# Weights of a fused attention and gated-unit kernel: float32 loads on SyncE's queue with casts on GpSimd in place of casting transfers, under another written order

## The chip, the cores and the metric

The kernel runs on one core of a Trainium2 chip. The metric is the device time of the program in microseconds (us): before the change 173.61, the median of three runs (173.09 to 173.88). Lower is better.

## The reference

Two stages follow each other. The first is causal attention for 4 batches, 8 heads, 768 positions and head size 64. Keys are grouped in chunks of 32, and each query keeps only the six chunks with the highest upper bound of its score:

```
ub = sum(max(q*k_min, q*k_max), axis=-1)       # for every query and chunk
top_chunks = argsort(ub)[..., -6:]             # causal chunks only
scores = where(chunk in top_chunks and causal, q@k.T / 8, -1e9)
attn = softmax(scores) @ v
```

The second stage takes the attention output, joined over the heads to x of [4, 768, 512], through a causal convolution of five taps per channel, which gives a gate, and through two 512 by 512 weights:

```
gate = sigmoid(sum(conv_w[k] * shifted(x, k) for k in range(5)))
out = (gate * (x @ w_val)) @ w_out
```

All inputs and the output are float32.

## The kernel before

**Tiles and stages.** Two heads are one pair, so there are 16 pairs p, and four pairs make a batch b. For each pair, K and Q are loaded (`Lk`, `Lq`, two transfers each) and transposed on TensorE (`KT`, `QT`); ScalarE copies them out of PSUM as float16 (`KE` L661, `QH` L701); VectorE reduces the chunk bounds (`KX` L672), and GpSimd prepares them (`KB`, `KS`, L680 to L697). TensorE multiplies the bounds (`CF`, `BD` L776), VectorE finds the sixth largest (`T8` L784, `CM` L791), and the mask reaches the score layout through a transposing DMA on SyncE's queue (`MD` L807) or, for the first pairs, through TensorE (`MT`). The scores of a pair are six blocks (`S` L819 to L824), each with two exponentials on ScalarE (`E` L828, 192 in all); GpSimd cuts the causal triangles (`A` L839) and casts V to float16 (`VC` L760); TensorE multiplies with V (`AV` L848), and VectorE normalises (`RC` L854, `NR` L864 or L870).

**The second stage.** The normalised rows are transposed for the second stage by a DMA on SyncE's queue (`XT` L890; pairs 0, 1 and 15 through TensorE). For the first two pairs of a batch the convolution is done on TensorE (`CV` L942), for the other two by five taps per pair (`TP`: the first on ScalarE, L925, four on VectorE, L928). `TH` (L932, L947) is the gate's tanh on ScalarE. `VL` is x @ w_val on TensorE, in a first half from the weights `wv` (L963) and a second, `z`, from `wvn` (L956). `GV` (L968) multiplies gate and value on VectorE, `OU` (L976) multiplies with the weights `wo`, `OE` (L984 on ScalarE, L986 on VectorE) copies the result into one of eight buffers `OSB` of 128 by 512 float32, and `ST` (L989) stores it.

**The weights.** They lie in SBUF as float16 and are loaded once, by twelve transfers from GpSimd's queue that cast while they move: `wval` (four, L1072) fills the lower 64 partitions of `wv`, `wvn` (four, L1066), and `wout` (four, L1081 and L1084). Two more transfers on SyncE's queue, `wvd0` and `wvd1` (L1075), copy the lower half of `wv` to the upper 64 partitions:

```
g.op("SP", 430, 430, f"wvd{j}", lambda js=js: nc.sync.dma_start(
    out=wval_sb[HP[1], js, 0:DM], in_=wval_sb[HP[0], js, 0:DM]),
     [("wv", 0, j, 0), ("wv", 0, j, 1)], [("wv", 1, j)], (), dma=700.0)
```

**What sets the order.** Nothing is scheduled when the program is built: each operation has a name, and `ORDER` (L110), a list of 1507 names written out in the file, is the order in which they are emitted. Every engine, and every engine's DMA queue, works through its share of that list strictly in turn and waits at the first operation whose inputs are not there. The transfers of SyncE's queue use eight semaphores in rotation, so each also waits until the eighth transfer before it has landed. The names `F` and `G` with a number are filler products on TensorE, without use for the result, that run while the first loads are on their way.

Of the kernel before, what the change touches and what calls it, by code (L numbers as in the profile page):

```python
# [110 lines left out]
Lk0.1 mfz F5 F14 F11 G6 mKB0 F13 cwl G11 G7 F7 F8 Lk0.0 F9 F6 ident identh G19 G2 G12 G15 KT0.1  # L111
KX0.10 KT0.0 KX0.00 G18 F0 mNS1 KX0.01 KX0.11 Lq0.1 QT0.1 QF0.1 mKF0 KF0.10 KF0.11 cwn0 F15 KF0.01
RF0.1 Lk2.0 cwn1 G14 cwt F4 em0 Lq0.0 cws F10 F12 Lk1.0 KF0.00 G16 G8 cfill ident2 QH0.1 KT2
KX2.11 identb CF0 BF0.3 T80.3 KE2.0 QT0.0 QF0.0 KX2.10 mNS0 KE2.1 G17 em1 G13 KX2.01 BF0.4 KX2.00
Lq2.0 BF0.5 T80.5 G5 T80.4 Lq1.0 G9 KE0.1 CM0.4 CM0.3 F2 QH0.0 KB2.0 KS2 KB2.1 KB2.2 CM0.5 dg01
KT1 KX1.00 RF0.0 BF0.2 em2 BF0.1 KX1.10 KX1.11 T80.2 mVA0 KE0.0 G3 G4 QT2 KE1.0 G0 T80.1 CM0.1 F3
KE1.1 CM0.2 Lk3.0 KX1.01 KB1.0 KS1 KB1.1 G10 F1 G1 QH2.1 QL2.1 MT0 ME0 QH2.0 QL2.0 dg03 RH2 QT1
QH1.0 mKB1 KB2.3 QL1.0 QH1.1 S0.5 E0.05 E0.15 S0.4 E0.14 KB1.2 KB1.3 E0.04 QL1.1 RH1 Lq3.0 S0.2
E0.12 S0.3 E0.13 Lk4.0 A0.4 Lv0 KT3 KB1.4 E0.02 S0.0 E0.10 CF1 BD1.5 BD1.4 BD1.2 KX3.10 BD1.3
E0.03 KX3.00 BD1.1 dg02 S0.1 CF2 KX3.11 KB2.4 BD2.2 BD2.1 T81.1 BD2.5 BD2.4 T81.3 E0.00 QT3 E0.01  # L120
E0.11 T81.5 A0.1 T81.4 KE3.1 T81.2 CM1 T82.4 QH3.0 KX3.01 KB3.0 KB3.1 MT1 ME1 QH3.1 Lq4.0 T82.5
KE3.0 S1.5 S1.4 A0.5 Lv1 E1.15 A0.3 KS3 KB3.2 KB3.4 QL3.0 E1.05 E1.04 Lv2 BD2.3 S1.1 QL3.1 RH3
E1.14 mVA1 KB3.3 E1.11 T82.3 Lk5.0 S1.3 E1.03 VC0 T82.2 T82.1 CM2 KT4 KX4.10 KX4.00 E1.13 S1.2
E1.12 A1.3 E1.01 KX4.01 KX4.11 S1.0 KB4.0 CF3 BD3.5 E1.10 VC1 BD3.2 Lq5.0 BD3.3 KE4.0 BD3.4 BD3.1
T83.1 A1.1 AV0.00 AV0.04 AV0.03 Lv3 T83.5 MT2 ME2 A1.4 KE4.1 KS4 mxT T83.4 AV0.12 T83.2 AV0.15
T83.3 AV0.10 AV0.11 AV0.05 AV0.13 AV0.14 RC0.1 AV0.02 AV0.01 RC0.0 E1.00 E1.02 A1.5 mVA2 CM3 S2.5
E2.15 E2.05 NR0.0 NR0.1 QT4 QH4.0 QL4.0 QH4.1 S2.1 Lk6.0 QL4.1 E2.11 E2.01 RH4 KB4.1 S2.3 E2.03
AV1.10 AV1.02 AV1.11 AV1.13 AV1.14 AV1.01 AV1.12 VC2 AV1.00 AV1.04 AV1.15 RC1.1 E2.13 AV1.03 S2.0
Lv4 NR1.1 KT5 E2.10 KX5.00 KX5.10 Lq6.0 A2.1 E2.00 KX5.11 S2.4 E2.04 E2.14 S2.2 KB4.2 E2.02 AV1.05
MT3 KB4.4 RC1.0 ME3 NR1.0 KE5.1 E2.12 KB4.3 CF4 BD4.1 BD4.2 BD4.3 XT0 XTE0 dg00 BD4.4 BD4.5 T84.5  # L130
S3.5 E3.15 E3.05 T84.3 Lk7.0 S3.1 E3.11 QT5 QH5.0 S3.2 A2.5 A2.3 A2.4 T84.4 AV2.05 AV2.02 T84.1
T84.2 KX5.01 CM4 KB5.0 KS5 AV2.01 AV2.04 E3.12 E3.02 QL5.0 AV2.03 AV2.00 RC2.0 KE5.0 E3.01 AV2.13
AV2.12 NR2.0 AV2.10 AV2.11 AV2.14 AV2.15 RC2.1 XT1 XTE1 S3.4 QH5.1 S3.3 NR2.1 E3.04 E3.03 XT2
# [6 lines left out]
AV3.05 E4.10 AV3.02 KX7.00 KX7.10 KB7.0 T86.5 KS7 T86.1 AV3.03 T86.2 QT7 RC3.0 T86.3 KB7.1 wvd0  # L140
T86.4 AV3.12 E4.13 QH7.1 A4.4 NR3.0 KB7.2 AV3.15 A4.5 AV3.11 AV3.10 AV3.14 QH7.0 KB7.4 CM6 KE7.1
KB7.3 QL7.1 AV3.13 RC3.1 QL7.0 KE7.0 NR3.1 S5.0 E5.00 wout0 S5.3 E5.13 XT3 RH7 E5.10 VC4 S5.1
E5.11 wvn3 TP2.4 KT8 S5.5 E5.05 E5.15 CF7 BD7.1 BD7.4 BD7.3 E5.01 T87.1 T87.4 E5.03 S5.4 E5.04
KX8.00 E5.14 S5.2 E5.02 E5.12 A4.3 AV4.15 KX8.11 KX8.10 MD6 AV4.14 BD7.5 BD7.2 AV4.10 AV4.13
AV4.12 KE8.1 KX8.01 Lk9.0 AV4.11 A5.5 T87.5 AV4.05 AV4.04 AV4.03 Lk10.0 RC4.1 T87.3 T87.2 AV4.01
AV4.02 KB8.0 KS8 TP3.0 KE8.0 AV4.00 NR4.1 RC4.0 VL0.1 A5.3 CM7 MD7 NR4.0 A5.4 TP3.1 QT8 QH8.0
QH8.1 VL0.1z GV0.11 GV0.10 TH2 S6.1 E6.01 QL8.1 QL8.0 S6.4 E6.04 VC5 A5.1 AV5.14 AV5.10 E6.14
AV5.15 AV5.03 AV5.11 AV5.01 AV5.02 AV5.13 AV5.04 Lq9.0 AV5.00 AV5.05 RC5.0 RH8 wout2 S6.5 E6.05
KB8.1 KB8.2 KB8.4 E6.15 A6.5 E6.11 wout3 Lq10.0 AV5.12 RC5.1 S6.3 E6.13 NR5.0 S6.0 E6.03 S6.2
E6.02 E6.12 TP3.2 NR5.1 TP3.3 VL0.2 VL0.2z GV0.20 E6.00 TP3.4 S7.3 E6.10 E7.13 A6.3 KT9 KX9.10  # L150
VL0.3 KX9.11 E7.03 GV0.21 TH3 S7.0 E7.00 wout1 VL0.3z CF8 KE9.1 KB8.3 BD8.2 BD8.4 BD8.1 GV0.30
# [998 lines left out]
```

## Time and profile before

| | us |
|---|---|
| median of three runs (lowest, highest) | 173.61 (173.09, 173.88) |
| the profiled execution, its own time | 173.19 |
| span of its trace, first to last instruction | 171.5 |
| busy: TensorE, VectorE, ScalarE, GpSimd | 159.6, 145.7, 145.3, 99.2 |
| granted TensorE clock | 0.999 of full speed |
| SyncE's queue: share of 16 DMA engines, MB | 79.7%, 29.96 |
| GpSimd's queue: share of 16 DMA engines, MB | 4.4%, 1.06 |

All times come from one profiled execution and count from the span's start. A row of the timeline gives start, duration, engine, source line, what is written from what, the number of instructions in the row, and, in brackets, how long the engine stood idle before it and what ended that. PE is TensorE, ACT ScalarE, DVE VectorE, POOL GpSimd, SP SyncE; SPq and POOLq are the instruction queues that issue transfers. The chain of waits follows the work that ended last back through whatever released each step; it is inferred from semaphore events. A busy TensorE is not a TensorE at its peak, since its products are pipelined.

### The profile page before, as it was taken

How to read it: one execution, taken by the hardware profiler on the slowest of the kernel's cores; microseconds unless marked ns; L12 is line 12 of the kernel's file. 1: busy time of each engine (PE TensorE's matmuls, PEld its weight loads, DVE VectorE, ACT ScalarE, POOL GpSimd, SP SyncE). 2: the span in 40 equal slices, each digit the busy share in tenths (PEclk: the TensorE clock that was granted, in tenths of full speed). 3: DMA queues.
4: the chain of work that ended last, by engine and by line, in shares of the span. 5: the costliest groups of instructions: out<-in, count | busy, mean ns of one | idle time of the engine just before them, and what ended most of it. 6: DMA issues, size and time to landing. Idle time of an engine off the chain costs nothing.

```text
span 171.5 us, 7644 instructions
## 1 busy us (share of the span) xinstructions
PE 159.6 (93%) x3118; PEld 106.7 (62%) x3118; DVE 145.7 (85%) x434; ACT 145.3 (85%) x320; POOL 99.2 (58%) x218
## 2 busy tenths in 40 slices
...
GB/s 98 222 271 190 268 252 268 230 64 99 216 143 194 177 196 209 257 134 201 165 202 150 214 254 204 185 129 184 202 113 237 272 185 2 74 85 207 166 191 237
DMA packets 98578, 31.50 MB, mean 184 GB/s; under 512 B 94187, under 2 KB 95467, under 8 KB 98544
## 3 DMA queue, kind: packets, MB, share of 16 engines
q1 hardware_dynamic: 97424, 29.96, 79.7%
q0 software_dynamic: 1120, 1.06, 4.4%
...
q14 instruction: 10, 0.08, 0.2%
...
## 4 chain that ended last, share of the span: by engine, by line
PE 40%; ACT 21%; DVE 16%; POOL 8%; DMA 7%; issue 3%; SPq 2%; POOLq 0%; ACTq 0%
ACT P L828 14%; PE ps L976 10%; DVE G L928 7%; PE ps L848 6%; PE ps L821 4%; PE ps L963 4%; PE ps L956 4%; PE ps L824 4%; PE ps L647 3%; DMA xT<-ON 3%; DVE GV L968 3%; ACT KE L661 3%; DMA QM<-NS 2%; POOL P L839 2%; DVE KK L672 2%
## 5 line engine op out<-in xcount | busy, mean ns | idle before, releaser
L828 ACT ACTIVATE P<-ps 128x512 f16<-128x512 f32 (+1 forms) x192 | 89.7, 582 | 5.0 <-PE ps L824 3.1
L839 POOL TENSOR_SCALAR_AFFINE_SELECT P<-P 128x256 f16<-128x256 f16 (+1 forms) x64 | 37.0, 591 | 21.5 <-ACT P L828 19.9
L824 PE MATMUL ps<-QM,EM 64*128 64x512 f16 (+4 forms) x256 | 36.6, 290 | 1.0 <-DMA QM<-NS 0.7
L672 DVE TENSOR_REDUCE KK<-ps 128x12 f32<-128x384 f32 x64 | 31.9, 547 | 4.8 <-PE ps L639 3.8
L821 PE MATMUL ps<-QHL,KE 64*128 64x512 f16 (+4 forms) x256 | 35.0, 292 | 0.2
L928 DVE SCALAR_TENSOR_TENSOR G<-xT,cwT,G 128x768 f32<-128x768 f16 x32 | 34.0, 1081 | 1.3 <-ACT G L925 1.2
L848 PEld LDWEIGHTS <-P 128*128 128x128 f16 x672 | 24.3, 98 | 8.7 <-issue 5.0
L848 PE MATMUL ps<-VA,P 128*128 128x65 f16 x672 | 27.8, 194 | 0.8 <-DVE GV L968 0.4
L976 PE MATMUL ps<-wo,GV 128*128 128x512 f16 (+1 forms) x100 | 23.1, 371 | 0.0
L821 PEld LDWEIGHTS <-KE 64*128 64x128 f16 x256 | 13.2, 94 | 7.9 <-issue 3.7
L661 ACT ACTIVATE KE<-ps 128x384 f16<-128x384 f32 x32 | 16.3, 550 | 0.9 <-DVE KK L672 0.9
L784 DVE MAX8 TOP<-ps 128x8 f32<-128x20 f32 (+4 forms) x160 | 15.6, 164 | 1.4 <-PE ps L776 1.4
L984 ACT ACTIVATE OSB<-ps 128x512 f32<-128x512 f32 (+1 forms) x22 | 13.0, 615 | 4.2 <-PE ps L976 4.2
L968 DVE SCALAR_TENSOR_TENSOR GV<-G,ps 128x384 f16<-128x384 f32 x32 | 16.2, 544 | 0.2
L760 POOL CAST VA<-vn 128x768 f16<-128x768 f32 x16 | 14.7, 916 | 3.0 <-DMA vn<-in_v_dram 2.9
L701 ACT ACTIVATE QHL<-ps 128x384 f16<-128x384 f32 x32 | 15.3, 537 | 0.8 <-PE ps L821 0.6
L824 PEld LDWEIGHTS <-EM 64*128 64x128 f16 x256 | 12.3, 94 | 4.3 <-issue 2.9
L741 DVE SCALAR_TENSOR_TENSOR QHL<-ps,QHL 128x320 f16<-128x320 f32 x30 | 13.6, 478 | 1.4 <-ACT QHL L701 1.4
L976 PEld LDWEIGHTS <-GV 128*128 128x128 f16 x100 | 8.7, 97 | 9.7 <-DVE GV L968 1.0
L776 PE MATMUL ps<-KB,RHL 128*128 128x48 f16 x225 | 13.2, 183 | 1.0 <-DVE RHL L748 0.5
L776 PE MATMUL ps<-KB,QHL 128*128 128x48 f16 x225 | 13.2, 183 | 0.0
L963 PE MATMUL ps<-xT,wv 64*128 64x384 f16 x128 | 13.1, 323 | 0.1
...
## 6 DMA issues: line engine op xcount, KB each, us to landing
...
```

Of the source, the lines that this page charges most:

```text
L661: nc.scalar.activation(out=spread(KE[p % 3], p, w), in_=bank(gr, None), func=AF.Copy)
L672: nc.vector.tensor_reduce(out=o, in_=i, axis=AX.X, op=ALU.min if mx else ALU.max)
L776: nc.tensor.matmul(out=o, lhsT=lt, rhs=kb[:, j, :], start=False, stop=(n == 5), skip_group_check=True)
L821: nc.tensor.matmul(out=pq[hh][:, col + a:col + n], lhsT=KE[p % 3][HP[hh], ks], rhs=QH[p % 3][HP[hh], q0 + a:q0 + n], start=True, stop=False)
L824: nc.tensor.matmul(out=pq[hh][:, col + a:col + n], lhsT=EM[HP[hh], ks], rhs=qm[HP[hh], q0 + a - 128:q0 + n - 128], start=False, stop=True)
L828: e.EX = lambda p, hh, bi, tot, gr: nc.scalar.activation(out=PT[hh, bi, p % 2][:, 0:tot], in_=bank(gr, None)[:, 0:tot], func=AF.Exp, scale ...
L839: nc.gpsimd.affine_select(out=ap, in_=ap, pattern=[[0, 2], [0, n], [1, 128]], compare_op=ALU.is_ge, fill=0.0, base=0, channel_multiplier=-1)
L848: nc.tensor.matmul(out=pav[:, qt, :], lhsT=PT[a, bi, p % 2][:, col:col + 128], rhs=VA[p % 3][:, hh, jt, :], start=(jt == 0), stop=(jt == qt))
L928: en.scalar_tensor_tensor(out=GT[sl], in0=x, scalar=w, in1=GT[sl], op0=ALU.mult, op1=ALU.add)
L963: nc.tensor.matmul(out=pv[h], lhsT=wval_sb[HP[h], gi, ws], rhs=xT[HP[h], (b % 2) * 2, gi, :, LD:LD + 128], start=(gi == 0), stop=False)
L968: e.GV = lambda b, et, w, gr: nc.vector.scalar_tensor_tensor(out=GVT[(b % 2) * NCT + et][:, w * HB:(w + 1) * HB], in0=GT[(b % 2) * NCT + e ...
L976: nc.tensor.matmul(out=po[:, 0:z - a], lhsT=GVT[(b % 2) * NCT + et][:, s * 128:(s + 1) * 128], rhs=wout_sb[:, et, a:z], start=(et == 0), s ...
```

## The change

The casting transfers and the two copies are gone. Ten loads on SyncE's queue bring the weights as float32, 256 KB each, into the buffers `OSB`, which hold nothing until the first output rows are ready, and ten casts on GpSimd write the float16 tiles. `WLa` (four loads) bring the part of w_val for `wv` twice, into the lower and the upper 64 partitions, and `CWa0` to `CWa3` cast it; `WLn` and `CWn` (two each) do `wvn`; `WLo` and `CWo` (four each) do `wo`, the last two of them in buffers that `CWa0` and `CWa1` have emptied. The first half of `VL` now waits for all four `CWa`, every `OU` for all four `CWo`. `wv` loses 32 unused columns, the eight `OSB` become one tile with eight parts, and `XT` and `XTE` must now follow `mxT`, which clears four columns ahead of each row.

```
-            g.op("SP", 430, 430, f"wvd{j}", lambda js=js: nc.sync.dma_start(
-                out=wval_sb[HP[1], js, 0:DM], in_=wval_sb[HP[0], js, 0:DM]),
...
+        def stage(name, out, in_, slots):
+            g.op("SP", 430, 430, name, lambda: nc.sync.dma_start(out=out, in_=in_), (),
+                 [("osb", i, a) for i in slots for a in (0, 256)], (), dma=700.0)
+
+        def cast(name, out, slot, key):
+            g.op("POOL", 600, 650, name, lambda: nc.gpsimd.tensor_copy(out=out, in_=OSB[slot]),
+                 [("osb", slot, 0), ("osb", slot, 256)], [key], ())
...
+        for x in range(2):
             for r in range(2):
+                rows = slice(64 * x + 32 * r, 64 * x + 32 * r + 32)
+                g.op("SP", 430, 430, f"WLa{x}{r}", lambda rows=rows, r=r: nc.sync.dma_start(
+                    out=OSBT[rows, 0:NG], in_=wsrc[r][:, 0:NG]), (), [("wst", x, r)], (), dma=700.0)
+        for n in range(NG):
+            g.op("POOL", 600, 650, f"CWa{n}", lambda n=n: nc.gpsimd.tensor_copy(
+                out=wval_sb[:, n], in_=OSB[n]), [("wst", x, r) for x in range(2) for r in range(2)],
+                 [("wv", n), ("osb", n, 0), ("osb", n, 256)], ())
+        for r in range(2):
+            stage(f"WLn{r}", OSB[NG + r], moe_w_val[256 + 128 * r:][0:128], [NG + r])
+            cast(f"CWn{r}", wval_nat[:, r], NG + r, ("wvn", r))
+        for j in range(NCT):
...
+            slot = (6, 7, 0, 1)[j]
+            stage(f"WLo{j}", OSB[slot], rows, [slot])
+            cast(f"CWo{j}", wout_sb[:, j], slot, ("wo", j))
```

The list `ORDER` is another one throughout, with 1513 names. Two of its new lines:

```
+BF0.2 KX1.00 KE2.0 QH0.0 F7 KE1.1 WLn1 KS2 KE1.0 QT2 KB2.2 KB2.3 T80.2 T80.1 CM0.2 F11 QH2.0 CM0.1
+MT0 QT1 QH2.1 KX1.10 ME0 G6 S0.2 QH1.1 Lv0 QH1.0 KX1.01 KB1.0 KB1.1 QL2.0 Lq3.0 E0.02 QL1.1 QL2.1
```

Three places of it follow, engine by engine as the built programs have them. The changed file's lines stand one lower than the old ones from L630 to L1056 (the transposes are L806 and L889 there); L1064 is `stage`, L1068 `cast`, L1078 `CWa`.

SyncE's queue around the transpose of pair 3, `XT3`, written from ON_133 to xT, with the mask transpose of pair 6 (QM_90) behind it. Names in brackets are the semaphores that a transfer waits for: DMAHW the eighth transfer before it, DMASW GpSimd's transfers, PE, DVE and Pool the engines. Before:

```order
L1075 DMA wv_66<-wv_66 64x2x512 [waits DMAHW1_49,DMASW2_49,DMASW1_49]
L1075 DMA wv_66<-wv_66 64x2x512 [waits DMAHW2_49,DMASW5_49,DMASW3_49]
L890 DMA_TRANSPOSE xT<-ON_133 128x6x128 [waits DMAHW3_49,DVE_49]
L807 DMA_TRANSPOSE QM_90<-NS_114 128x5x128 [waits DMAHW4_49,PE_49]
L630 DMA kn_76<-in_k_dram 128x6x64 [waits DMAHW5_49]
```

Now:

```order
L1064 DMA OSB<-in_moe_w_out_dram 128x512 [waits DMAHW6_49]
L629 DMA kn_77<-in_k_dram 128x6x64 [waits DMAHW7_49,PE_49]
L629 DMA kn_77<-in_k_dram 128x6x64 [waits DMAHW0_49]
L625 DMA vn_85<-in_v_dram 128x12x64 [waits DMAHW1_49,Pool_49]
L625 DMA vn_84<-in_v_dram 128x12x64 [waits DMAHW2_49]
L889 DMA_TRANSPOSE xT<-ON_133 128x6x128 [waits DMAHW3_49,DVE_49]
L1064 DMA OSB<-in_moe_w_out_dram 128x512 [waits DMAHW4_49,Pool_49]
L806 DMA_TRANSPOSE QM_90<-NS_114 128x5x128 [waits DMAHW5_49,PE_49]
```

The two copies that waited for GpSimd's transfers ahead of `XT3` are replaced by loads; behind `XT3` stands a load, `WLo3`, that waits for GpSimd (for the cast `CWa1`), and the mask of pair 6 stands behind that.

GpSimd from the bounds of pair 7 (KK_105) to the last triangle of pair 4 (the P_0 tiles). Before, with the last of the `wvn` transfers and the first `wout`:

```order
L680 TENSOR_TENSOR KK_105<-KK_105 128x24
L695 TENSOR_SCALAR KQ_107<-KK_105 128x48
L684 TENSOR_SCALAR KC_109<-KK_105 128x48
L839 AFFINE_SELECT P_0_120<-P_0_120 128x2x128
L697 TENSOR_TENSOR KC_109<-KQ_107,KC_109 128x48
L839 AFFINE_SELECT P_0_121<-P_0_121 128x256
L692 COPY KB_111<-KC_109 64x4x24 x2
L1084 DMA wo_68<-in_moe_w_out_dram 64x1024
L760 CAST VA_95<-vn_83 128x12x64
L1066 DMA wvn<-in_moe_w_val_dram 64x512
L839 AFFINE_SELECT P_0_119<-P_0_119 128x2x256
```

Now:

```order
L679 TENSOR_TENSOR KK_105<-KK_105 128x24
L694 TENSOR_SCALAR KQ_107<-KK_105 128x48
L683 TENSOR_SCALAR KC_109<-KK_105 128x48
L696 TENSOR_TENSOR KC_109<-KQ_107,KC_109 128x48
L691 COPY KB_111<-KC_109 64x4x24
L838 AFFINE_SELECT P_0_119<-P_0_119 128x2x256
L838 AFFINE_SELECT P_0_121<-P_0_121 128x256
L1078 CAST wv_66<-OSB 128x512 x2
L691 COPY KB_111<-KC_109 64x4x24
L838 AFFINE_SELECT P_0_117<-P_0_117 128x4x128
L1078 CAST wv_66<-OSB 128x512 x2
```

The four `CWa` casts stand between the parts of pair 7's bounds and the triangles of pair 4, where transfers were issued before.

ScalarE around the first tap of pair 3 (`TP3.0`, which reads what `XT3` wrote). Before, behind the last exponential of pair 5:

```order
L828 ACTIVATE P_1_124<-ps_1760 128x512
L661 ACTIVATE KE_89<-ps_1703 128x6x64
L925 ACTIVATE G_137<-xT,cwT 128x768
L661 ACTIVATE KE_89<-ps_1702 128x6x64
L701 ACTIVATE QHL_99<-ps_1863 128x6x64
L701 ACTIVATE QHL_99<-ps_1864 128x6x64
L932 ACTIVATE G_136<-G_136 128x768
```

Now:

```order
L827 ACTIVATE P_1_126<-ps_1714 128x512
L660 ACTIVATE KE_89<-ps_1687 128x6x64
L827 ACTIVATE P_1_125<-ps_1722 128x512
L700 ACTIVATE QHL_99<-ps_1843 128x6x64
L700 ACTIVATE QHL_99<-ps_1842 128x6x64
L924 ACTIVATE G_137<-xT,cwT 128x768
L931 ACTIVATE G_136<-G_136 128x768
```

The tap moved behind one more copy of K and both copies of Q.

More of the change, by code (lines that the diff above doesn't have):

```diff
@@ L110 @@
 ORDER = """
[L111 to L133, printed above, removed]
@@ L140 @@
[L140 to L151, printed above, removed]
@@ L206 @@
-ST3.0 OU3.2 OE3.2 ST3.2 OU3.3 OE3.3 ST3.3 OU3.4 OE3.4 ST3.4 OU3.5z OE3.5z ST3.5z OU3.5 OE3.5 ST3.5
+cwl Lk0.1 mKB1 Lk0.0 mfz mxT F12 G11 F13 F10 G5 G14 F4 G9 F9 ident identh F3 G17 F5 cfill Lq0.1
+F15 G16 KT0.1 KT0.0 KX0.11 ident2 mNS0 G12 Lk2.0 KE0.1 cwn0 QT0.1 QF0.1 RF0.1 G7 F8 Lq0.0 QH0.1
+KX0.10 cwn1 KX0.01 cwt F6 mKF0 KX0.00 KF0.10 Lk1.0 cws mKB0 KF0.00 F1 KT2 F14 KF0.01 KF0.11 KX2.10
+KX2.11 Lq2.0 KX2.00 Lq1.0 KE0.0 identb CF0 BF0.3 BF0.5 BF0.4 mVA0 KE2.1 T80.5 T80.3 T80.4 QT0.0
+QF0.0 CM0.3 em0 em1 CM0.5 F2 CM0.4 dg00 em2 G3 KX2.01 KB2.0 F0 KB2.1 KT1 RF0.0 BF0.1 Lk3.0 KX1.11
```

185 lines of the change are left out of this document (98 added, 87 removed).

## The prediction, made before the change had run

> **What bounds the kernel now.** I read the page first, then the list of waits, the chain, and the timelines of single engines where the chain leaves TensorE and ScalarE.
>
> ```profile
> span 171.5 us, 7644 instructions
> PE 159.6 (93%) x3118; PEld 106.7 (62%) x3118; DVE 145.7 (85%) x434; ACT 145.3 (85%) x320; POOL 99.2 (58%) x218
> 40.00:50.00 10.00, 8.57 (x295) 6.27 (x295) 9.41 (x26) 9.68 (x24) 8.54 (x19) 1.00 1.01 183
> 50.00:60.00 10.00, 9.07 (x191) 6.80 (x188) 8.87 (x39) 8.83 (x21) 9.33 (x21) 1.00 0.91 166
> ```
>
> No engine is the bound by itself: three are filled to 85% or more, so a bubble that they share is the thing to look for. The two rows by stage (us, then busy PE, PEld, DVE, ACT, POOL, the clock, DMA) show one: between 40 and 60 us GpSimd, elsewhere at 58%, is busy 8.54 and 9.33 of 10, and the others have holes. Here is the chain of waits (start, length, what) in that stretch, cut:
>
> ```profile
> 44.50 0.58 POOL wv L1072
> 47.57 0.51 POOL wv L1072
> 48.50 0.49 POOL wvn L1066
> 48.99 0.55 POOL wv L1072
> ...
> 54.88 4.74 DMA xT<-ON
> 59.64 0.94 ACT G L925
> ```
>
> It runs through the very transfers that the change removes, to XT3, and from there to the tap TP3.0 on ScalarE. Why XT3 starts at 54.88 is in SyncE's queue, in its waits, and in the row of VectorE that completes XT3's input:
>
> ```profile
> 50.78 4.00 SPq L1075 DMA_DIRECT2D wv<-wv  x2
> 54.88 1.78 SPq L890 DMA_TRANSPOSE xT<-ON  x1
> 56.75 1.23 SPq L807 DMA_TRANSPOSE QM<-NS  x1
> SPq L1075 <- DMA wv<-in_moe_w_val_dram: 2.6, 1, 2.6
> 52.69 0.54 DVE L864 TENSOR_TENSOR ON<-ps,RCP 128x384 f16<-128x384 f32 x1
> ```
>
> The rows of pair 3 are ready at 52.69 + 0.54 = 53.23, but the queue is held by the second weight copy, which waits 2.6 us for a casting transfer from GpSimd and is issued only by 54.78. XT3 starts 54.88 - 53.23 = 1.65 us late, and its transfer lands at 59.62. Who pays:
>
> ```profile
> 59.64 0.94 ACT L925 ACTIVATE G<-xT,cwT 128x768 f32<-128x768 f16 x1 [1.06 <-DMA xT<-ON]
> 60.61 1.28 DVE L928 SCALAR_TENSOR_TENSOR G<-xT,cwT,G 128x768 f32<-128x768 f16 x1 [0.92 <-ACT G L925]
> 61.01 0.26 PE L819 MATMUL ps<-QHL,KE 64*128 64x192 f16 x2 [0.61 <-ACT KE L661]
> ```
>
> ScalarE idles 1.06 us, VectorE 0.92 us behind it, TensorE 0.61 us: one bubble on all three, and it hangs on the two copies.
>
> **The change part by part.** *The copies go.* With no wait for GpSimd in SyncE's queue, XT3 can be issued when its rows are ready, 1.65 us earlier, more than the 1.06 us that ScalarE waits; in the new order TP3.0 also stands behind three further copies on ScalarE. So the bubble closes: -1.06 us. Next late there is XT3's own length: 53.23 + 4.74 = 57.97, against a ScalarE that reaches the tap at 59.64 - 1.06 = 58.58.
>
> *GpSimd.* Transfers out, casts in:
>
> ```profile
> L760 POOL CAST VA<-vn 128x768 f16<-128x768 f32 x16 | 14.7, 916 | 3.0 <-DMA vn<-in_v_dram 2.9
> L1072 POOL DMA_DIRECT2D wv<-in_moe_w_val_dram x4 | 2.4, 600 | 0.0
> L1066 POOL DMA_DIRECT2D wvn<-in_moe_w_val_dram x4 | 2.1, 537 | 0.0
> L1081 POOL DMA_DIRECT2D wo<-in_moe_w_out_dram x2 | 1.3, 626 | 0.0
> L1084 POOL DMA_DIRECT2D wo<-in_moe_w_out_dram x2 | 1.1, 574 | 0.0
> ```
>
> Removed: 2.4 + 2.1 + 1.3 + 1.1 = 6.9 us. No cast of 128x512 is in the trace; the nearest row is the cast of V, 916 ns for 768 columns, so 0.61 us by columns (0.54 us if it is no cheaper than an issued transfer, 0.92 us if width does not matter). Ten are 6.1 us (5.4 to 9.2). GpSimd's sum is thus almost unchanged; what changes is that nobody on SyncE waits for it, and that the casts are spread from pair 1 to pair 7. I take 0, from -0.5 to +1.0 us.
>
> *SyncE's queue and the DMA engines.* Two copies less, ten loads more. By shape a load is 256 KB, 2.5 MB in all, for 1.06 MB of casting transfers and 0.25 MB of copies before, over 31.5 MB. Where a load stands ahead of work with spare time it costs nothing. The place with least spare is the start, where WLn1 and Lv0 now stand ahead of Lq3, the Q of pair 3:
>
> ```profile
> 12.06 1.30 SPq L630 DMA_DIRECT2D qn<-in_q_dram  x2
> 16.27 0.59 SPq L626 DMA_DIRECT2D vn<-in_v_dram  x1
> DMA to landing us min/median/max: 2.3/3.5/6.3
> 20.50 0.58 PE L647 MATMUL ps<-ident,qn 64*128 64x64 f32 x12
> ```
>
> Lq3 (12.06) and the next load up to Lv0 (16.27) are four issues in 4.21 us, 1.05 each. Two more ahead make Lq3 2.1 us later: issued by 12.06 + 1.30 + 2.1 = 15.46, landed 3.5 to 6.3 later, 18.96 to 21.76 (median and maximum of the Q loads). Its transposes began at 20.50, so the cost is 0 by the median, +1.3 us at worst. I take 0.
>
> *The new wait.* The first half of VL needs all four CWa, and the scores of pair 6 stand behind VL on TensorE, their exponentials behind those. From the new order, after VectorE has the bounds of pair 7:
>
> ```profile
> 48.30 1.94 DVE L672 TENSOR_REDUCE KK<-ps 128x12 f32<-128x384 f32 x4
> L680 POOL TENSOR_TENSOR KK<-KK 128x24 f32<-128x24 f32 x15 | 3.8, 251 | 14.4 <-DVE KK L672 14.1
> L692 POOL COPY KB<-KC 64x96 f16<-64x96 f16 x30 | 10.9, 365 | 1.4
> L839 POOL TENSOR_SCALAR_AFFINE_SELECT P<-P 128x512 f16<-128x512 f16 x32 | 23.0, 724 | 7.5 <-ACT P L828 6.5 <-POOL P L839 0.6
> L839 POOL TENSOR_SCALAR_AFFINE_SELECT P<-P 128x256 f16<-128x256 f16 x32 | 14.6, 458 | 14.0 <-ACT P L828 13.5
> 58.45 0.82 PE L963 MATMUL ps<-xT,wv 64*128 64x384 f16 x8
> ```
>
> The bounds end at 50.24. Then come six small operations (0.25 to 0.37, say 2.0 in all), two wide triangles (1.45), a narrow one (0.46) and four casts (2.44): 50.24 + 6.35 = 56.6. VL began at 58.45, so 1.8 us are left: cost 0 as long as the casts are not held up.
>
> *The written order* moves everything else too. Up to about 45 us ScalarE is full and its queue keeps the same content, so I expect nothing there. Behind 60 us the trace bounds what other waits can give or take:
>
> ```profile
> ACT P L828 <- PE ps L824: 3.1, 5, 1.1
> ACT P L828 <- POOL KB L692: 1.3, 1, 1.3
> ```
>
> That is 4.4 us of waits of the exponentials. An order can remove a part or add as much; I take 0, with 1.0 us either way. `XT` behind `mxT`, the dropped columns and the joined OSB are free: nothing in the new order waits more for them, since mxT now stands at the start.
>
> *Sum*, on the profiled execution, 1.69 us of whose 173.19 lie around the span: 173.19 - 1.06 = 172.13. That execution is 0.42 under the median of the three runs; from the median the sum is 172.55. I put 172.4 between them.
>
> **The rivals.** *The copies were not all that held it (about the same).* For: TensorE waited only 0.61 us, and behind 62 us the chain is mostly products. If TensorE's bubble is what counts, 173.19 - 0.61 = 172.58, with the same allowance of 0.27 for the median 172.85. Against: VectorE waited 0.92 us for the same cause and is as full as ScalarE.
>
> *The casts are held up (slower).* Small copies on GpSimd take long beside a tap on VectorE, while an issued transfer did not:
>
> ```profile
> 42.28 0.26 POOL L692 COPY KB<-KC 64x96 f16<-64x96 f16 x1
> 46.08 1.00 DVE L928 SCALAR_TENSOR_TENSOR G<-xT,cwT,G 128x768 f32<-128x768 f16 x1
> 46.18 1.02 POOL L692 COPY KB<-KC 64x96 f16<-64x96 f16 x1
> 47.31 1.07 DVE L928 SCALAR_TENSOR_TENSOR G<-xT,cwT,G 128x768 f32<-128x768 f16 x1
> 47.51 0.56 POOL L1072 DMA_DIRECT2D wv<-in_moe_w_val_dram  x1
> ```
>
> The copy of 0.26 us takes 1.02, until just past the tap's end at 47.08; the transfer inside the next tap takes 0.56, about its mean. So the change swaps work that is not held for work that may be. If each CWa loses up to a tap, 1.0 us, the last ends at 56.6 + 4.0 = 60.6, VL starts 2.2 us late, and TensorE and ScalarE with it: 173.19 - 1.06 + 2.2 = 174.3, with the allowance 174.6. It decides from 58.4 on. Against: three of the four taps of pair 2 stand ahead of the bounds of pair 7 in the new order, so the casts meet one tap, or two. [...]
>
> *More goes (faster).* If the new order also saves a quarter of the 4.4 us, 1.1 us, it is 172.4 - 1.1 = 171.3.
>
> **How the numbers follow.** A measurement of this kernel tells about 0.5% from no change, 0.87 us, so "faster" is under 172.74 and "slower" over 174.48. The forecast, the bubble closed and little else, has 0.44: 0.36 of it faster, 0.08 the same, since its edge of a few tenths reaches 172.74. TensorE's bubble alone has 0.20, the same. More gain has 0.11, faster. The held casts, with the late Lq3 as a smaller case of its kind, have 0.25: 0.22 slower, 0.03 the same. Faster 0.47, same 0.31, slower 0.22. The range takes in the two outer rivals, 171.3 and 174.6, and leaves what lies beyond them, about two in ten: 171.2 to 174.6. The likeliest case alone spans 171.9 to 172.9.
>
> **What would show it.** Right: no wait of SyncE's queue for GpSimd's transfers, XT3 issued within 0.3 us of its rows, no wait of TP3.0 over 0.3 us, casts of 0.55 to 0.70 us, VL not waiting for a cast. Wrong: VL or OU waiting for GpSimd; the transposes of pair 3's Q waiting for their load; casts of 1 us and more; or TP3.0 on time and the waits of ScalarE and TensorE behind 60 us grown by the same microsecond.

## The result and the profile after

The change made the kernel slower. Before: median 173.19 us (172.68 to 175.51, 20 runs). After: median 176.82 us (173.33 to 181.91, 20 runs). The ratio is 1.0113, with a 95% interval of 1.0076 to 1.015. After's runs lie 5% apart and before's 1.6%, and the ratio leaves out every run more than 1.5% above its kernel's fastest (it keeps five of after's twenty), so the medians of all runs stand beside it here and below.

The profiled execution of after is its fastest, 173.33 us, hardly over the 173.19 us of before's. It shows where after stops, not all that its usual runs lose; two of those follow under after_again_1 and after_again_2. The page, with DMA queues as packets, MB and share of 16 engines:

```profile
span 171.6 us, 7644 instructions
PE 160.9 (94%) x3118; PEld 108.6 (63%) x3118; DVE 145.7 (85%) x434; ACT 145.3 (85%) x320; POOL 99.6 (58%) x216
...
q1 hardware_dynamic: 98576, 32.32, 88.4%
```

The engines have as much work as before (TensorE 1.3 us more, at a clock of 0.987). What has grown is SyncE's DMA queue: 88.4%, where both data queues together had 84.1% (79.7 and 4.4). The stages, in the columns of the prediction:

```profile
40.00:50.00 10.00, 8.04 (x257) 5.25 (x252) 8.60 (x24) 8.91 (x22) 6.96 (x13) 0.89 1.01 217
50.00:60.00 10.00, 9.88 (x223) 7.49 (x219) 8.91 (x40) 9.26 (x23) 5.76 (x13) 0.94 1.12 228
```

The hole has moved forward: 40 to 50 us now holds 257 products where 295 stood, at a clock of 0.89. The place that the prediction looked at is mended, here in the timeline (VectorE's normalising row, `XT3`, the last casts `CWa2` and `CWa3`, the next `MD`, the first half of `VL`, `TP3.0`, then TensorE and ScalarE behind it):

```profile
54.95 0.55 DVE L863 TENSOR_TENSOR ON<-ps,RCP 128x384 f16<-128x384 f32 x1
55.53 1.54 SPq L889 DMA_TRANSPOSE xT<-ON  x1
55.70 1.16 POOL L1078 CAST wv<-OSB 128x512 f16<-128x512 f32 x2
57.82 1.20 SPq L806 DMA_TRANSPOSE QM<-NS  x1
59.41 0.89 PE L962 MATMUL ps<-xT,wv 64*128 64x384 f16 x8
60.38 1.12 ACT L924 ACTIVATE G<-xT,cwT 128x768 f32<-128x768 f16 x1
62.53 0.39 PE L823 MATMUL ps<-QM,EM 64*128 64x512 f16 x2 [1.15 <-DMA QM<-NS]
63.00 1.09 ACT L827 ACTIVATE P<-ps 128x512 f16<-128x512 f32 x2 [0.78 <-PE ps L823]
```

The rows are ready at 55.50 and `XT3` is issued at 55.53; the tap has no bracket, so ScalarE did not wait for it. But the rows themselves come 2.3 us later than before, and behind the tap there is a new wait of TensorE, 1.15 us for a mask (`MD6`), with one of 0.78 us on ScalarE behind it. The larger stop lies earlier, where SyncE's queue carries three of the four `WLa` (the first went out at 32.67), V of pair 4, K of pair 8 and Q of pair 7:

```profile
40.16 1.05 SPq L1075 DMA_DIRECT2D OSB<-in_moe_w_val_dram  x2
41.31 0.39 SPq L625 DMA_DIRECT2D vn<-in_v_dram  x1
41.73 1.58 SPq L1075 DMA_DIRECT2D OSB<-in_moe_w_val_dram  x1
43.36 1.75 SPq L629 DMA_DIRECT2D kn<-in_k_dram  x2
45.16 3.44 SPq L629 DMA_DIRECT2D qn<-in_q_dram  x2
47.70 0.88 PE L646 MATMUL ps<-ident,kn 64*128 64x64 f32 x12 [1.39 <-ACT P L827]
47.81 0.90 POOL L759 CAST VA<-vn 128x768 f16<-128x768 f32 x1 [1.19 <-DMA vn<-in_v_dram]
```

TensorE stands for 1.39 us ahead of K's transposes of pair 7, GpSimd 1.19 us for V, and issuing the two loads of `Lq7` takes 3.44 us. Some transfers land later: the medians from issue to landing are 5.4 us for V, 3.5 for `XT` and 4.1 for `MD`, where the same view of before has 4.8, 2.8 and 3.4. Only V's goes with the loads. old_path_new_order below, which has the new order without them, reads 4.8, 3.5 and 4.3, and the loads of K and Q of 192 KB land no later than before (3.7 and 3.9 us against 3.9 and 4.2).

### The profile page after: what moved, and what is told of

It reads as the page before. It is cut to its first block, busy times and chain, and to the rows that moved or that the text cites. A ratio compares the mean times of both kernels' runs of the same rounds, so it can differ in the third digit from the quotient of the medians.

```text
span 171.6 us, 7644 instructions
## 1 busy us (share of the span) xinstructions
PE 160.9 (94%) x3118; PEld 108.6 (63%) x3118; DVE 145.7 (85%) x434; ACT 145.3 (85%) x320; POOL 99.6 (58%) x216
## 3 DMA queue, kind: packets, MB, share of 16 engines
q1 hardware_dynamic: 98576, 32.32, 88.4%
## 4 chain that ended last, share of the span: by engine, by line
PE 50%; DVE 19%; ACT 15%; DMA 9%; issue 3%; SPq 1%; DVEq 0%
ACT P L827 10%; PE ps L975 8%; DVE G L927 6%; PE ps L820 6%; PE ps L847 6%; DMA QM<-NS 5%; PE ps L823 5%; PE ps L955 5%; PE ps L962 4%; PE ps L646 4%; PE ps L775 3%; DVE KK L671 3%; DMA xT<-ON 3%; PE ps L941 2%; DVE TOP L783 2%
## 5 line engine op out<-in xcount | busy, mean ns | idle before, releaser
L827 ACT ACTIVATE P<-ps 128x512 f16<-128x512 f32 (+1 forms) x192 | 91.1, 577 | 6.8 <-PE ps L823 6.7
L838 POOL TENSOR_SCALAR_AFFINE_SELECT P<-P 128x512 f16<-128x512 f16 (+1 forms) x64 | 37.5, 599 | 27.2 <-ACT P L827 26.2
L823 PE MATMUL ps<-QM,EM 64*128 64x512 f16 (+4 forms) x256 | 38.1, 293 | 1.9 <-DMA QM<-NS 1.9
L820 PE MATMUL ps<-QHL,KE 64*128 64x512 f16 (+4 forms) x256 | 35.9, 295 | 0.9 <-DVE QHL L740 0.9
L927 DVE SCALAR_TENSOR_TENSOR G<-xT,cwT,G 128x768 f32<-128x768 f16 x32 | 34.7, 1104 | 0.3
L820 PEld LDWEIGHTS <-KE 64*128 64x128 f16 x256 | 13.8, 96 | 7.0 <-issue 2.9
L783 DVE MAX8 TOP<-ps 128x8 f32<-128x12 f32 (+4 forms) x160 | 15.3, 162 | 1.4 <-PE ps L775 1.0
L775 PE MATMUL ps<-KB,RHL 128*128 128x48 f16 x225 | 13.9, 184 | 0.4 <-DVE TOP L783 0.4
L775 PE MATMUL ps<-KB,QHL 128*128 128x48 f16 x225 | 13.8, 184 | 0.0
L775 PEld LDWEIGHTS <-RHL 128*128 128x128 f16 x225 | 11.5, 97 | 3.0 <-issue 2.3
```

What stands on the lines that cost most here:

```text
L775: nc.tensor.matmul(out=o, lhsT=lt, rhs=kb[:, j, :], start=False, stop=(n == 5), skip_group_check=True)
L783: nc.vector.max(out=TOP[p % 2][:, it - 1, s, :], in_=bank(gr, None)[:, it - 1, s * NCH:s * NCH + n])
L820: nc.tensor.matmul(out=pq[hh][:, col + a:col + n], lhsT=KE[p % 3][HP[hh], ks], rhs=QH[p % 3][HP[hh], q0 + a:q0 + n], start=True, stop=False)
L823: nc.tensor.matmul(out=pq[hh][:, col + a:col + n], lhsT=EM[HP[hh], ks], rhs=qm[HP[hh], q0 + a - 128:q0 + n - 128], start=False, stop=True)
L827: e.EX = lambda p, hh, bi, tot, gr: nc.scalar.activation(out=PT[hh, bi, p % 2][:, 0:tot], in_=bank(gr, None)[:, 0:tot], func=AF.Exp, scale ...
L838: nc.gpsimd.affine_select(out=ap, in_=ap, pattern=[[0, 2], [0, n], [1, 128]], compare_op=ALU.is_ge, fill=0.0, base=0, channel_multiplier=-1)
```

## The experiments

Where an edit only moves names in `ORDER`, the diff shows the names around the place. Each ratio is against before, run beside it on the same chip. Where medians of two jobs are compared, before's own median differs between them, from 172.82 to 173.42 us.

### Which part: bubble, order or weight path

**old_path_copies_later.** Before, with the two copies behind `XT3`.

```
-AV3.00 wvd1 AV3.05 ... KB7.1 wvd0 T86.4 ... XT3 RH7
+AV3.00 AV3.05 ... KB7.1 T86.4 ... XT3 wvd1 wvd0 RH7
```

> The kernel before, with only its two copies wvd1 and wvd0 moved on SyncE's queue to just behind XT3, so that XT3 no longer waits behind a copy that waits for GpSimd's casting transfers; nothing else is changed. Theory of the prediction (the shared bubble at 58.6 to 61 us is on every engine's path): XT3 is issued 1.6 us earlier, the tap TP3.0 waits no more, and the time falls by 0.9 to 1.2 us, to 172.0 to 172.3 beside 173.2. Rival (only TensorE's 0.6 us was on the path, or the gain is given back at the next transfer): 172.6 to 173.2.

Median 173.94 us, ratio 1.0062 (1.0038 to 1.0086). Its timeline at `XT3`, `TP3.0` and `VL`:

```profile
53.40 2.11 SPq L888 DMA_TRANSPOSE xT<-ON  x1
58.56 0.96 ACT L923 ACTIVATE G<-xT,cwT 128x768 f32<-128x768 f16 x1
60.22 0.82 PE L961 MATMUL ps<-xT,wv 64*128 64x384 f16 x7 [1.30 <-DMA wv<-wv]
```

The bubble closes as the prediction worked out (`XT3` 1.5 us earlier, the tap at 58.56 without a wait), and the gain is given back at once: `VL` waits 1.30 us for the copy that now comes last. The time even rises, from 172.99 to 173.94, so no price of the bubble can be read from this run.

**new_path_old_order.** After's loads and casts put into before's order, each near the transfer that it replaces.

```
-S3.1 ... wval10 ... wval11 ... wval01 ... wval00 wvn2
+WLa11 S3.1 ... WLa01 ... WLa00 ... WLa10 ... CWa0 ... CWa1 ... CWa2 CWa3
```

> The kernel after with the written order of the kernel before: the ten float32 loads stand in SyncE's queue and the ten casts on GpSimd, but every other instruction stands where it stood before. Theory O (the new written order costs the time): 171.9 to 172.9, as the prediction had it for the weight path alone, with runs within 1% of each other and a granted clock of 0.99 or more. Theory Q (ten more loads in SyncE's queue hold up its other transfers, by more or less from run to run): 175 to 178, with runs that differ by 2% or more, as the kernel after.

Median 180.5 us, ratio 1.0449 (1.0425 to 1.0473). GpSimd's timeline shows why it says nothing about the order:

```profile
50.86 0.61 POOL L1076 CAST wv<-OSB 128x512 f16<-128x512 f32 x1 [5.97 <-DMA OSB<-in_moe_w_val_dram]
```

The casts stood too early, and GpSimd, with the bounds of the next pairs behind it, waited 5.97 us for a load. It does show what a cast costs that waits on GpSimd.

**old_path_new_order.** After's order with before's transfers and copies.

```
-XTE1 A3.4 ... CM5 E4.00 ... S4.3 CF6 ... Lv5 AV3.14
+XTE1 wval10 A3.4 ... CM5 wval11 E4.00 ... S4.3 wval00 wvn2 CF6 ... Lv5 wvd1 wvd0 AV3.14
```

> The kernel before (casting transfers on GpSimd, two copies on SyncE) with the written order of the kernel after; the transfers stand between the instructions beside which they stood before, the two copies ahead of XT3. Theory O: 175 to 178 with runs that differ by 2% or more, as the kernel after, and KT7 waits on TensorE at 47 us. Theory Q: 172 to 174 with runs within 1%.

Median 173.04 us (171.25 to 174.26), ratio 0.9979 (0.9948 to 1.001). So the order alone costs nothing, and what after loses comes with the weight path. Its stages read

```profile
40.00:50.00 10.00, 8.51 (x286) 5.85 (x284) 8.66 (x27) 9.56 (x23) 9.25 (x19) 1.00 1.13 184
50.00:60.00 10.00, 9.04 (x187) 6.33 (x184) 9.35 (x39) 8.89 (x22) 6.63 (x15) 1.00 1.18 229
```

with DMA shares (1.13 and 1.18) above those of after (1.01 and 1.12): a full share by itself did not make this kernel slow. Its queue at the place of the stop, for comparison (Lk8, then Lq7):

```profile
40.43 1.78 SPq L628 DMA_DIRECT2D kn<-in_k_dram  x2
42.26 1.28 SPq L628 DMA_DIRECT2D qn<-in_q_dram  x2
```

**kt7_behind_s43.** After, with K's transposes of pair 7 behind the next scores, since these had their inputs.

```
-S4.4 KT7 KX7.10 WLo0 S4.3 CF6
+S4.4 WLo0 S4.3 KT7 KX7.10 CF6
```

> The kernel after with pair 7's key transposes (KT7) and the reduction KX7.10 put behind pair 4's score products S4.3 instead of ahead of them. Theory O in its narrow form (TensorE's wait of 1.39 us for a PSUM bank at KT7, with S4.3 behind it, and the stretch of lower granted clock that follows): 1.0 to 2.5 us less than the kernel after, 174 to 176 in the median, and the granted clock stays at 1.00 from 40 to 60 us. Rivals (the wait moves to the next bank, or the spread comes from the loads in SyncE's queue): within 0.5 us of the kernel after, runs still 2% and more apart.

Median 176.3 us, ratio 1.0157 (1.0112 to 1.0202). The list of waits of TensorE:

```profile
PE ps L817 <- ACT P L826: 1.7, 1, 1.7
```

The stop did not go with the transposes. It stayed at the same place in TensorE's stream, now ahead of `S4.3`, 1.72 us long. So neither K nor Q of pair 7 was what TensorE stood for there (the last section comes back to it).

### Where the four WLa stand

**wla_early.** All four at the first one's place; `Lq8` later, to make room.

```
-RC1.0 WLa11 NR1.0 Lq8.0 S3.1 ... MD5 E4.10
+RC1.0 WLa11 WLa01 WLa00 WLa10 NR1.0 S3.1 ... MD5 Lq8.0 E4.10
```

> The kernel after, with the four loads WLa taken out of the stretch from 40 to 46 us: three of them follow the first in SyncE's queue, at 33 to 36 us, where Lq8 stood, and Lq8 goes behind MD5, to 49 us. What the runs so far show: with the old weight path the new order takes 173.0 us and TensorE's clock stays at 1.00; in the kernel after, and in the one with KT7 behind S4.3, TensorE stops at the same place of its stream of instructions (its 1729th record of the trace, whichever instruction stands there) with its semaphores long reached, starts again 1.2 to 1.4 us after a 16 KB transfer of the instruction queue has landed, and the granted clock is 0.5 for the next 3.4 us. Theory I (the WLa loads hold up the transfer that brings TensorE's instructions, while 160 short products of the convolution use up the instructions at hand; the stop costs 1.3 us and the halved clock some 1.7 us): the instruction transfer that starts at 45.5 us after starts by 44 us, no stop of over 0.5 us at 46 us, clock 1.00, median 172.5 to 174.0 and runs within 1.5%. Rival Q (it is the count and the bytes of the loads, wherever they stand, that delay the mask and row transfers): 175.5 to 177.5 with runs 2% and more apart.

**wla_late.** Three of them behind `MD5`.

```
-E3.14 WLa01 ... E3.03 WLa00 ... KB6.0 WLa10 ... MD5 E4.10
+E3.14 ... E3.03 ... KB6.0 ... MD5 WLa01 WLa00 WLa10 E4.10
```

> The kernel after, with three of the four loads WLa (01, 00, 10) put behind MD5 in SyncE's queue, at 49 to 52 us; their casts stay at 53.5 us and later. Theory I: the instruction transfer starts by 44 us, no stop of TensorE at 46 us, clock 1.00, Lv4 lands earlier and VC4 doesn't wait, median 172.5 to 174.0 and runs within 1.5%, unless the casts wait for the later loads (each 0.5 us of that 0.5 us more). Rival Q: 175.5 to 177.5 with runs 2% and more apart.

Early: median 176.87 us, ratio 1.0165 (1.0105 to 1.0225). Late: 177.22 us, ratio 1.0227 (1.0171 to 1.0284). Moving them helped neither time, and each place has its own late transfer. TensorE's waits in wla_early:

```profile
PE ps L954 <- DMA xT<-ON: 2.5, 1, 2.5
```

and in wla_late:

```profile
PE ps L822 <- DMA QM<-NS: 3.8, 3, 2.7
```

With the four early, issuing them takes 3.98 us and the late one is `XT3`; with three of them late, it is the masks.

**after_again_1** and **after_again_2** are after unchanged, one execution each, to see what its other executions look like.

> The kernel after once more, for a profile of one of its usual executions (its median is 176.8 us, the one profiled so far took 173.3). [...]

> [...]

175.47 us and 180.6 us. The first, in the timeline of SyncE's queue (the last `WLa`, Lk8, Lq7) and of TensorE:

```profile
43.55 0.74 SPq L1075 DMA_DIRECT2D OSB<-in_moe_w_val_dram  x1
44.34 3.61 SPq L629 DMA_DIRECT2D kn<-in_k_dram  x2
47.99 2.49 SPq L629 DMA_DIRECT2D qn<-in_q_dram  x2
53.59 0.58 PE L646 MATMUL ps<-ident,qn 64*128 64x64 f32 x12 [2.79 <-DMA qn<-in_q_dram]
```

The second of the two Lk8 issues took 3.09 us, though the semaphore that it needs had been reached 2.4 us before it began. Lq7 then goes out at 47.99, 5.7 us later than in old_path_new_order, lands at 53.45, and TensorE stands 2.79 us for it. Not all of that is lost behind the three `WLa`: the first of them went out at 41.97 us here and at 40.16 in the profiled execution above, so 1.8 us were lost earlier. The stage in the windows:

```profile
50.00:60.00 10.00, 7.21 (x135) 5.17 (x134) 6.32 (x24) 6.70 (x16) 6.77 (x15) 0.83 1.09 224
```

All engines have holes together, and the clock falls to 0.83 behind the stop. The second execution has two such stages, and its list of waits names two culprits:

```profile
PE ps L823 <- DMA QM<-NS: 4.7, 4, 2.4
PE ps L646 <- DMA qn<-in_q_dram: 2.4, 1, 2.4
```

So in each of the three profiled executions of after something between 45 and 66 us is late, and what it is differs from run to run.

### The loads by themselves

**no_wla.** After without the four `WLa`: it leaves out loading these weights, and the buffers are set to 0 at the start.

```
-WLa11 ... WLa01 ... WLa00 ... WLa10
+g.op("DVE", 2000, 2000, "WLa", lambda: nc.vector.memset(OSBT[:, 0:NG], 0.0), (),
```

> The kernel after without its four loads WLa: it leaves out loading the four slabs of the value weights (the slots are set to 0 at the start instead, and cast as before), everything else is as in the kernel after. What the runs so far show: in the usual executions of the kernel after, TensorE waits 2.4 to 2.8 us for Lq7 at 51 to 53 us and up to 2.4 us for MD6, after such a stop its clock is 0.5 for 3.4 us, and moving the WLa loads earlier or later only moves the wait to VL's rows or to MD6. Theory B (backlog: with 1.05 MB of WLa loads among the loads of K, Q and V the 16 DMA engines run behind from 40 to 60 us, the issue of the next loads in SyncE's queue takes up to 3 us, and Lq7, MD6 or XT3 land late): 171.3 to 173.3, runs within 1.5%, no wait for Lq7, clock 1.00. Theory G (the casts on GpSimd or the other six loads): 175 to 177.

Median 174.15 us (171.84 to 177.04), ratio 1.0004 (0.9972 to 1.0037): 2.7 us under after, still 1.3 over before's 172.85 in the same job by the medians. Its profiled execution is its longest, 177.04 us. It does not wait for Q of pair 7, but for masks:

```profile
PE ps L822 <- DMA QM<-NS: 4.5, 3, 2.3
```

So late masks, and a good part of the spread, come without the `WLa` too.

**old_path_plus_wla.** old_path_new_order with the four `WLa` added at after's places, into `OSB` joined as in after; nothing uses what they bring.

```
+                g.op("SP", 430, 430, f"WLa{x}{r}", lambda rows=rows, r=r: nc.sync.dma_start(
+                    out=OSBT[rows, 0:NG], in_=wsrc[r][:, 0:NG]), (),
+                     [("wst", x, r)], (), dma=700.0)
```

> The kernel before in the new order (173.0 us), with the four loads WLa added to SyncE's queue where the kernel after has them; what they load is used by nothing, the weights still come by the casting transfers. Theory B: 175 to 178, runs 2% and more apart, and waits for Lq7 or MD6 as in the kernel after. Theory G: 172.5 to 173.5.

Median 176.23 us, ratio 1.0115 (1.007 to 1.0159), against 0.9979 without them: 3.2 us by the medians, for loads on which nothing waits. In its profiled execution (177.8 us, above its median) the queue and TensorE's waits show after's picture again:

```profile
42.17 3.33 SPq L630 DMA_DIRECT2D kn<-in_k_dram  x2
45.55 3.76 SPq L630 DMA_DIRECT2D qn<-in_q_dram  x2
```

```profile
PE ps L647 <- DMA qn<-in_q_dram: 3.9, 1, 3.9
PE ps L647 <- ACT P L828: 1.8, 1, 1.8
```

This shows the cause most plainly. No cast is in it, no other order, and nothing that waits for the loads; they take only their bytes, their issues and four places among the eight semaphores. The same two pairs of issues that took 1.78 and 1.28 us take 3.33 and 3.76, and Q of pair 7 costs TensorE 3.9 us.

**wla_on_gpsimd.** After's four `WLa` issued from GpSimd's queue, at the places of before's `wval`.

```
-                g.op("SP", 430, 430, f"WLa{x}{r}", lambda rows=rows, r=r: nc.sync.dma_start(
+                g.op("POOL", 1000, 1000, f"WLa{x}{r}", lambda rows=rows, r=r: nc.gpsimd.dma_start(
```

> The kernel after with the four loads WLa (same bytes, float32, no cast) issued by GpSimd instead of SyncE, where the kernel before had its casting transfers. Theory B (bytes and 16 DMA engines shared by both queues): 174.5 to 177.5, little less than the kernel after. Rival S (the place in SyncE's queue, whose other transfers stand behind the loads): 172 to 173.5, as the old path in the new order.

Median 175.53 us (173.14 to 178.34), ratio 1.0093 (1.0059 to 1.0128). Lq7 is issued at 42.70 now, and TensorE waits for masks instead:

```profile
PE ps L822 <- DMA QM<-NS: 5.4, 5, 2.2
```

So standing ahead of Lq7 in SyncE's queue was one way for the loads to do harm, and not the only one: from another queue, and at later places, they still cost (1.0093, against 1.0004 without them). That they do it by delaying the masks is not shown, since no_wla's profiled execution waits 4.5 us for masks without them.

**new_path_old_order_slack.** After's path in before's order once more: loads in gaps of SyncE's queue, casts late.

```
+Lk7.0 WLa11 WLa01 WLa00 WLa10 S3.1 ... Lq8.0 WLn1 WLn0 ... MD7 WLo0 ... Lq9.0 WLo1 ... Lq10.0 WLo2 WLo3
```

> The written order of the kernel before with the new weight path, the four loads WLa put at 34 to 38 us, where the kernel before has its DMA engines busy for a third of the time, the two loads WLn behind Lq8, the four WLo behind MD7 and Lq10, and the casts where the casting transfers stood or later. Theory B: the loads use idle engines, so 172.0 to 173.5 with runs within 1.5%, level with the kernel before or ahead of it by the bubble at 58.6 us. If the loads cost wherever they stand: 175 to 178.

Median 176.39 us (174.25 to 178.44), ratio 1.0114 (1.0074 to 1.0154), as expected if the loads cost wherever they stand. The four `WLa` go out from 34.33 us, and from 34 to 38 us the DMA share of before is 0.39; room there did not save the time (six other loads stand elsewhere). Its profiled execution, 174.25 us, has no TensorE wait over 1.1 us, so what its median stands for stays open. It does show that after's path is slow in two quite different orders.

**no_loads.** After without any of the ten loads; it leaves out bringing the weights (the buffers are set to 0), and the casts stay.

```
-WLn1 ... WLn0 ... WLa11 ... WLa01 ... WLa00 ... WLa10 ... WLo0 ... WLo3 ... WLo1 ... WLo2
+g.op("DVE", 4000, 4000, "WLz", lambda: nc.vector.memset(OSBT, 0.0), (),
```

> The kernel after without any of its ten loads of weights: it leaves out loading them (the eight rows' buffers are set to 0 at the start), the ten casts stay. Leaving out the four WLa alone took the median from 176.8 to 174.2 us. Theory B (the transfers alone cost, the casts nothing): 171.5 to 173.2, as the old path in the new order (173.0), runs within 2%. Rival C (the casts, or GpSimd's later order, hold the last 1.1 us): 174 to 174.6, as without the four WLa.

Median 171.51 us (170.95 to 174.87), ratio 0.9908 (0.9883 to 0.9933). The page and the windows:

```profile
span 169.8 us, 7628 instructions
...
q1 hardware_dynamic: 97136, 29.70, 79.2%
```

```profile
40.00:50.00 10.00, 9.32 (x301) 6.40 (x298) 9.55 (x24) 9.97 (x23) 6.84 (x13) 1.00 0.73 156
50.00:60.00 10.00, 9.53 (x184) 6.54 (x181) 9.93 (x41) 9.99 (x23) 7.68 (x16) 1.00 0.93 188
```

ScalarE is full in both stages, the clock is whole, and the DMA share between 40 and 50 us is 0.73 where after has 1.01. It is 172.82 - 171.51 = 1.3 us faster than before. That lies near the 1.06 worked out, but it is not the kernel that was forecast: it moves no weights at all, neither by the ten loads nor by the old transfers (30.18 MB in all, before 31.50). The 1.3 us are order, casts, closed bubble and missing bytes together. The ten loads cost 176.82 - 171.51 = 5.3 us in the median (4.9 with each kernel against the before of its own job), about half of it (2.7, or 2.3) the four `WLa`.

**wla_quarter.** The four `WLa` cut to 128 of 512 columns; it leaves out loading the others, which are set to 0 at the start.

```
-                    out=OSBT[rows, 0:NG], in_=wsrc[r][:, 0:NG]), ...
+                    out=OSBT[rows, 0:NG, 0:128], in_=wsrc[r][:, 0:NG, 0:128]), ...
```

> The kernel after with its four loads WLa cut to the first 128 of 512 columns (64 KB each instead of 256 KB; it leaves out loading the other columns): as many loads, as many rows, a quarter of the bytes. If the cost of 2.7 us goes by the bytes: 174.3 to 175.2 (174.2 without the loads, plus a quarter). If it goes by the number of loads in SyncE's queue (issue, semaphores, the landing that the eighth load behind waits for): 176 to 177.5.

Median 174.46 us, ratio 1.0039 (1.0005 to 1.0073). As many issues as after, a quarter of their bytes, and the time is near that without them (174.15) and 2.4 us under after: most of the cost goes with the bytes, not with the number of issues.

**wla_once.** Each value slab loaded once; every `CWa` casts it into both halves of `wv`. The result is the same.

```
-        for x in range(2):
+        for x in range(1):
...
-            g.op("POOL", 600, 650, f"CWa{n}", lambda n=n: nc.gpsimd.tensor_copy(
+            g.op("POOL", 1200, 1250, f"CWa{n}", lambda n=n: [nc.gpsimd.tensor_copy(
```

> The kernel after with each slab of the value weights loaded once instead of twice (two loads WLa instead of four, 0.52 MB instead of 1.05), and each of the four casts CWa made twice, from the lower 64 partitions into the lower and into the upper 64: the same result with half the bytes and 2.4 us more on GpSimd. By the bytes: half of the 2.7 us comes back, 175.0 to 176.0. If the longer casts hold up GpSimd's masks ahead of VL: 176.5 to 178.

Median 174.04 us (172.82 to 175.47), ratio 1.0071 (1.0036 to 1.0106). Half of the `WLa` bytes gone is 2.8 us off after's median, four more casts included. Of the forms of the new path that leave nothing out it is the best, and it does not reach before. By the ratios the cost grows with the bytes of the `WLa`: 1.0004 with none of them, 1.0039 with a quarter, 1.0071 with half, 1.0113 with all. Neighbouring intervals overlap, and the medians (174.15, 174.46, 174.04, 176.82) do not show the steps between.

### Attempts at a faster kernel

**new_order_wvn_later.** old_path_new_order with its `wvn` transfers later (and `wval00` earlier, right behind `wval01`), so that the bounds of pair 6 need not wait behind them on GpSimd.

```
-KT7 wvn1 KX7.10 S4.3 wval00 wvn2 CF6 ... S4.1 wvn0 VC4 ... KB7.4 S5.5
+KT7 KX7.10 S4.3 CF6 ... S4.1 VC4 ... A4.4 wvn1 wvn2 KX7.00 ... KB7.4 wvn0 S5.5
```

> The old weight path in the new order (173.0 us) with three of the casting transfers, wvn1, wvn2 and wvn0, behind the key bounds of pair 6 on GpSimd instead of among them, and wval00 ahead of those. In that run TensorE waited 0.91 us at 48.2 us for those bounds, and GpSimd's five transfers from 43.1 to 46.4 us stood ahead of them. If that wait is on the path and nothing else is late: 172.0 to 172.4, ahead of the kernel before by 0.4 to 0.6%. If the next wait takes its place: 172.8 to 173.3.

Median 174.5 us, ratio 1.0027 (0.9987 to 1.0066): no faster. In its list of waits the next late transfer is the copy that `VL` needs:

```profile
PE ps L961 <- DMA wv<-wv: 2.4, 1, 2.4
```

**once_and_order** and **order_only.** wla_once, and after, each with `Lv4` ahead of `WLa01`, Lq7 ahead of Lk8, and `WLo0` and `WLo3` later.

```
-E3.14 WLa01 ... A3.3 Lv4 ... S4.5 Lk8.0 ... KS6 Lq7.0 ... KX7.10 WLo0 ... BD7.3 WLo3
+E3.14 Lv4 WLa01 ... A3.3 ... S4.5 Lq7.0 ... KS6 Lk8.0 ... Lq9.0 WLo3 ... WLo1 WLo0
```

> The kernel with each value slab loaded once (two loads WLa, double casts; 174.0 us), with three changes to SyncE's order: Lv4 ahead of the WLa loads, Lq7 ahead of Lk8 (QT7 is due at 50 us, KT8 at 55), and WLo0 and WLo3 behind Lq9 instead of ahead of Lk10 and MD6. In the profile of that kernel TensorE waited 1.0 us for Lq7 at 50 us, and WLo3's issue of 0.6 us stood ahead of MD6. Theory B, with the order of need: 172.6 to 173.6, level with the kernel before. If the four loads WLo in a row only move the backlog to Lq10 and Lk11: 174 to 175.5.

> The kernel after with the same three changes to SyncE's order, but all four WLa loads and single casts. Theory B (what counts is the bytes ahead of a transfer that is due): the wait for Lq7 goes, as Lk8 takes its place behind, 1 to 2 us less than the kernel after, 174.8 to 176; the runs stay 2% apart. If the order of SyncE's queue were the whole cause: 172.5 to 173.5.

177.52 us, ratio 1.0211 (1.0161 to 1.0262), and 180.57 us: both worse than what they were to mend. In order_only masks are late:

```profile
PE ps L822 <- DMA QM<-NS: 5.2, 4, 3.8
```

The longest of these waits ends at 83.25 us. The four `WLo`, now close together, had gone out at 65.70 to 67.60, so that they made this mask late is not shown.

The profiled execution of once_and_order says nothing of this: there twelve transposes took 0.90 or 0.91 us up to 19.7 us and 0.59 from 21.96 us on, where wla_once's took 0.58 or 0.59 from 7.55 us on, and the scores of pair 0 began at 19.95 us where all others have 13.9 to 15.3. Its clock is shown as full there; that it was half is an estimate from after, whose twelve transposes at a granted clock of 0.50 took 0.88 us (the row at 47.70). Why that kernel's median is high stays open. No kernel with its loads in place beat before beyond its interval.

## Why the prediction was wrong, point by point

**The bubble: its waits right, its price not shown.** What it named of the queue came true: no wait for GpSimd's transfers is left in it, `XT3` goes 0.03 us behind its rows, `TP3.0` does not wait. old_path_copies_later shows by itself that moving the copies closes the bubble. That this is worth 1.06 us no run shows: there the time rose, and the 1.3 us of no_loads hold the missing bytes too, so that they come near is luck as far as is known.

**The casts: right.** Forecast 0.61 us each. By shape, with count, sum and mean:

```profile
L1068 POOL CAST wo<-OSB 128x512 f16<-128x512 f32 x4 | 3.0, 756 | 0.1
L1078 POOL CAST wv<-OSB 128x512 f16<-128x512 f32 x4 | 2.3, 608 | 0.0
L1068 POOL CAST wvn<-OSB 128x512 f16<-128x512 f32 x2 | 1.2, 605 | 0.0
```

One `wo` cast took 1.21 us, twice the others, and it ran beside a tap on VectorE:

```profile
65.92 1.10 DVE L927 SCALAR_TENSOR_TENSOR G<-xT,cwT,G 128x768 f32<-128x768 f16 x1
66.28 1.21 POOL L1068 CAST wo<-OSB 128x512 f16<-128x512 f32 x1
```

None of the other nine met a tap. So casts can be held as that rival had it, but no product of after waited for a cast: the rival named the right sign for another reason.

**The new wait: right.** The last `CWa` ended at 55.70 + 1.16 = 56.86 (forecast 56.6), and `VL` began at 59.41 without waiting for it.

**The written order: right within its allowance.** Forecast 0, 1.0 us either way; old_path_new_order measured 0.9979 (0.9948 to 1.001).

**SyncE's queue and the DMA engines: the step that failed.** It read "Where a load stands ahead of work with spare time it costs nothing. The place with least spare is the start", and took 2.5 MB of loads at 0, +1.3 at worst. Lq3 there was indeed free: in its profiled execution after's TensorE waits at most 0.2 us in sum for K or Q loads. But the price of a transfer is not only its slot in the queue. Measured, the ten loads cost 5.3 us in the median, and old_path_plus_wla gives 3.2 for the four `WLa` in a kernel that does not use them; most of it goes with their bytes. The likeliest way is that from 40 to 60 us the DMA engines had no spare time (the prediction's own rows read 1.01 and 0.91 in the column that was not used), so that further bytes push back transfers that share the engines. That way is argued, not shown: old_path_new_order reads 1.13 and 1.18 there and loses nothing, and new_path_old_order_slack loses as much as after with its `WLa` where before's engines had room.

**The last line of "what would show it" came closest.** It named `TP3.0` on time with waits behind 60 us grown; after has 1.15 us on TensorE and 0.78 on ScalarE there. The larger stop, at 46.31 to 47.70 us, lies between the 45 us up to which the prediction expected nothing and the 60 us behind which it gave its allowance.

**The range** left out the case that happened. Its slow end priced one mechanism with a few tenths of spread; this change also widened the spread, from 1.6% to 5%, so that the fastest run (173.33) lies inside the range and the median outside.
